# A tuned attention-then-FFN kernel on one core: the steps of its opening put in a new order, from the thirteenth on

## The chip, the cores and the metric

The kernel runs on one core of one Trainium2 chip. The metric is the device time of one execution in microseconds (us); several executions are taken and their median is compared.

The engines go by short names in the profile: PE is TensorE, PEld its weight loads, DVE is VectorE, ACT is ScalarE, POOL is GpSimd, SP is SyncE, which here only issues transfers. "SPq", "ACTq" and "POOLq" are the instruction streams from which an engine issues a transfer (DMA).

## The reference: what is computed

Eight batches with eight heads each, 576 queries and keys of 64 numbers per head, and 16 "beacon" keys and values per head put in front of the keys. Attention is causal for the 576 keys, the beacons are seen by all queries. The result of all heads (4608 tokens of 512 numbers) goes through a feed-forward part with three first matrices, of which the largest of three products is kept.

```
scores = scale * (q @ concat(beacon_k, k).T)      # causal for k, not for the beacons
a      = exp(scores - max);  a /= sum(a)
x      = a @ concat(beacon_v, v)                  # B x S tokens, H x D numbers
h      = maximum(maximum(x @ w1, x @ w2), x @ w3) # 512 -> 768
out    = h @ w_out                                # 768 -> 512
```

## The kernel before, in words

**Units of work.** Two heads make a pair, numbered over all batches: pairs 0 to 3 are batch 0, pairs 4 to 7 batch 1, 8 to 11 batch 2. Two pairs (four heads) make a quad: quads 0 and 1 are batch 0. The work is issued in an order that is written out by hand as a list of steps, `first_steps` (line 897) for the opening and `loop_steps` (line 1073) for the rest. Nothing plans at run time: each step appends its instructions to the in-order streams of the engines that it uses, and the engines wait for each other only where data or a buffer demands it. So the order of two steps matters for each engine that both use, and does not matter for the others. A step that issues transfers appends them to SP's or to GpSimd's stream, where they also stand in order.

**The steps**, with the lines that the profile names:

- `("load half", p, i, queue)`, line 219: the first half of the queries (i=0) or keys (i=1) of a pair, by SP or ScalarE; `("cast half", p, i, engine)`, line 227, makes it bf16. `("load quad half", g, h)`, line 236: half h of a quad's queries and keys, two transfers from GpSimd's stream, which convert on the way. `("load quad", b, g)`, line 245: the same for whole rows of a quad of batch b; it feeds the pairs of that quad ("whole").
- `("half", p, h, bank, q_copy, idle, idle_q)`, line 423: turns a half with TensorE (12 transposes, line 435) into two PSUM banks and copies queries and keys to SBUF (line 443). The keys are always copied by VectorE, the queries by the engine `q_copy`. `bank` is "pv" or "ffn". `idle_q` and `idle` are numbers of pairs of empty transposes (line 403) put in front of the queries and of the keys; they keep TensorE running where it would wait. `("whole", p, bank, q_copy)`, line 795, does it for all rows of a pair (24 transposes, line 384; copies, lines 448 and 459).
- `("load keys", ...)`, `("cast keys", ...)`, `("turn keys", ...)`: beacon keys of batch 0 (set 0) and of batches 1 to 3 (set 1), cast (lines 862 and 876) and turned by TensorE (line 355); ScalarE copies them out of PSUM (lines 361 and 362). `("keys", p, engine)`, line 455, places them in front of a pair's keys.
- `("scores", p, group, idle)`, line 498: `idle` empty matmuls (line 473), then the score matmuls of one of four groups of a pair (line 509), then the exponential of both heads on ScalarE (line 524), into the tile `at_sb`. The PSUM tile comes from a ring of two buffers ("sc"); `("widen",)` closes the pool of the FFN banks and adds a third buffer ("wide") to the ring.
- `("mask", p, group, engine)`, line 530: sets what a query may not see to zero, with up to three instructions, each either a product with a triangle on VectorE or an affine_select on GpSimd:

```
if dve:
    m = tri[0:n, None, x0 : x0 + hi - lo]
    nc.vector.tensor_mul(view, view, m.to_broadcast([n, 2, hi - lo]))   # line 541
else:
    nc.gpsimd.affine_select(out=view, in_=view, ...)                     # line 543
```

- `("load v0", t, gate)`, line 293, and `("cast v0", t, engine)`, line 317: one of five pieces of batch 0's values from SP's stream, and its cast to bf16 (line 323). `("load v", b, piece, gate)` loads three or two pieces of a later batch. `("load pair", p, gate)` loads queries and keys of a pair of batch 2 from SP's stream (line 202).
- `("values", quad, half, bank, ...)`, line 563: the matmuls of probabilities with ones (which form the sums) and with values (line 584), 44 for a quad's first half of rows and 76 for its second. It needs every mask of its two pairs, and the casts of the value pieces that it reads. `("invert",)`, line 598: ScalarE forms the reciprocals of the sums (lines 604 and 606). `("multiply",)`, line 610: three VectorE products (line 616) put the result in `xT`.
- `("ffn", bank, kind)`, line 821: the next unit of the feed-forward part of a kind: 0 and 1 are the first and second 256 tokens of the first block of 512 tokens (eight matmuls, line 665, then VectorE, lines 673 and 675). Units 1 to 3 of kind 0 use w1 of the reference, units 4 to 6 w2, units 7 to 9 w3. `("load w", i)`, line 333, loads one of these, i = 0, 1, 2, with two transfers from GpSimd's stream. `("load w_out", gate)` loads the last matrix.
- `("load", n, gate)`: the next n loads of a list of later ones.

**The gates.** A load with a gate first writes one number of its target on the named engine. So the transfer can't start before that engine has come to this point of its stream:

```
def load_first_v(t, gate=None):
    dst = v_stage(0, t)
    if gate:
        idle[gate].memset(dst[32:33, 0, 0:1], 0.0)
    load_v_tile(0, t, dst)
```

All transfers of SP's stream stand in order, so one that waits for its gate also holds those behind it. GpSimd's own transfers have no gates; they are issued when GpSimd has done the steps in front of them.

**Around the change.** The first twelve steps are the same in both kernels: they load the halves of pairs 0 and 1, keep TensorE running with empty matmuls until the first data are there (about 7 us), and load the first halves of quad 1. After the opening, `loop_steps` goes over the batches in a fixed pattern; the change does not touch it.

## Time and profile before

| what | value |
|---|---|
| median of 3 runs | 291.97 us (291.77 to 292.08) |
| the profiled execution | 292.01 us, of which 289.6 us are the span of the instructions |
| TensorE busy | 279.8 us (97%), 3704 matmuls |
| VectorE, ScalarE, GpSimd busy | 168.2, 145.2 and 121.9 us |
| granted TensorE clock | 0.999 of full |
| transfers | 45.30 MB, 156 GB/s over the span |

The "timeline" view lists instructions in order of time, runs of alike ones merged: start and length in us, engine, line, operation, what is written <- what is read, shape, number, and in brackets how long the engine was idle before and what ended it. The "DMA" view gives for each queue its packets, MB and the time of its packets as a share of 16 DMA engines, and for each issue its size and the time to landing; q0 holds the transfers from GpSimd's stream and q1 those of SP's.

### The profile page before, as it was taken

To read this page: it belongs to the slowest core of one execution; us is meant where nothing else is said; L and a number is where in the kernel's file an instruction comes from. 1 tells how busy PE (TensorE), PEld (TensorE's weight loads), DVE (VectorE), ACT (ScalarE), POOL (GpSimd) and SP (SyncE) were. 2 spreads that over 40 slices of the span, in tenths; PEclk is the share of its full clock that TensorE was granted. 3 is DMA by queue.
4 is the path that set the end of the run, shared out by engine and by line. 5 is a ranking of instruction groups with operands and counts; after the bars stand their busy time and mean duration, and the time that the engine had idled before them with its cause. 6 is when DMAs were issued, how large, how long until landed. Compare 5 with 4: busy or idle time off the path is not lost.

```text
span 289.6 us, 8831 instructions
## 1 busy us (share of the span) xinstructions
PE 279.8 (97%) x3704; PEld 160.6 (55%) x3729; DVE 168.2 (58%) x317; ACT 145.2 (50%) x248; POOL 121.9 (42%) x246
## 2 busy tenths in 40 slices
PE   8889999999999999999999999999999999999995
PEld 7656677754555554544555887445554545444442
DVE  1555677856675557565746655665556565373273
ACT  2886576854566564835484258525862552200300
POOL 3717416644476483638365546464523320000000
PEclk9999999999999999999999999999999999999999
DMA  8999999999999999999999999999991003002103
GB/s 131 168 179 183 219 198 234 221 205 219 235 204 187 148 197 164 199 170 219 201 181 157 223 192 194 139 167 187 253 163 75 2 2 144 3 0 82 65 0 146
DMA packets 118231, 45.30 MB, mean 156 GB/s; under 512 B 107312, under 2 KB 112944, under 8 KB 118192
## 3 DMA queue, kind: packets, MB, share of 16 engines
q1 hardware_dynamic: 111984, 39.20, 76.1%
q0 software_dynamic: 5648, 5.21, 11.9%
q8 instruction: 29, 0.48, 0.7%
q10 hardware_dynamic: 560, 0.33, 0.4%
q14 instruction: 10, 0.08, 0.1%
HBM read 35.13 MB, written 9.44 MB: 154 GB/s over the span
## 4 chain that ended last, share of the span: by engine, by line
PE 86%; DMA 4%; ACT 3%; DVE 2%; POOL 2%; issue 1%; ACTq 0%; POOLq 0%
PE pv L646 21%; PE sc L646 14%; PE wide L646 8%; PE sc L682 8%; PE sc L584 7%; PE pv L682 6%; PE sc L509 6%; PE pv L584 5%; PE wide L509 3%; DMA w_sb<-in_moe_w_dram 2%; DMA bk<-in_beacon_k_dram 2%; PE wide L682 1%; PE pv L665 1%; PE wide L584 1%; PE sc L665 1%
## 5 line engine op out<-in xcount | busy, mean ns | idle before, releaser
L524 ACT ACTIVATE at_sb<-sc 128x736 bf16<-128x736 f32 (+5 forms) x87 | 72.9, 863 | 62.9 <-PE sc L509 62.3
L543 POOL TENSOR_SCALAR_AFFINE_SELECT at_sb<-at_sb 128x256 bf16<-128x256 bf16 (+3 forms) x140 | 51.7, 387 | 105.7 <-ACT at_sb L524 104.7
L646 PEld LDWEIGHTS <-w_sb 128*128 128x128 bf16 x648 | 61.1, 98 | 60.7 <-issue 4.9
L646 PE MATMUL pv<-xT,w_sb 128*128 128x512 bf16 (+1 forms) x315 | 65.2, 347 | 0.3
L524 ACT ACTIVATE at_sb<-wide 128x672 bf16<-128x672 f32 (+3 forms) x41 | 35.1, 856 | 23.3 <-PE wide L509 23.1
L646 PE MATMUL sc<-xT,w_sb 128*128 128x512 bf16 (+1 forms) x202 | 44.1, 362 | 0.3
L656 DVE TENSOR_TENSOR hT<-hT,pv 128x512 bf16<-128x512 bf16 x48 | 32.4, 686 | 13.2 <-PE pv L646 13.2
L255 POOL CAST p<-st 96x768 bf16<-96x768 f32 x48 | 38.3, 824 | 3.4 <-DMA st<-in_k_dram 3.4
L682 PEld LDWEIGHTS <-hT 128*128 128x128 bf16 x210 | 19.6, 98 | 23.5 <-issue 1.1
L616 DVE TENSOR_TENSOR xT<-pv,recip 128x288 bf16<-128x288 f32 (+2 forms) x48 | 14.2, 350 | 26.5 <-ACT recip L606 26.5
L509 PE MATMUL sc<-qT,kT 64*128 64x288 bf16 (+6 forms) x286 | 26.8, 271 | 2.0 <-POOL at_sb L543 0.6
L509 PEld LDWEIGHTS <-kT 64*128 64x128 bf16 x400 | 14.8, 94 | 22.2 <-issue 12.8
L646 PE MATMUL wide<-xT,w_sb 128*128 128x512 bf16 (+1 forms) x113 | 26.1, 364 | 0.5 <-issue 0.2
L584 PEld LDWEIGHTS <-v_sb 128*32 128x32 bf16 (+1 forms) x1408 | 24.7, 96 | 2.3 <-issue 1.0
L682 PE MATMUL sc<-w_out_sb,hT 128*128 128x512 bf16 x103 | 24.4, 379 | 0.3
L656 DVE TENSOR_TENSOR hT<-hT,sc 128x1024 bf16<-128x1024 bf16 (+1 forms) x15 | 17.0, 1147 | 5.2 <-PE sc L646 5.0
L682 PE MATMUL pv<-w_out_sb,hT 128*128 128x512 bf16 x83 | 19.9, 380 | 0.1
L656 DVE TENSOR_TENSOR hT<-hT,wide 128x1024 bf16<-128x1024 bf16 (+1 forms) x11 | 12.3, 1120 | 10.8 <-PE wide L646 10.6
L311 POOL CAST v_sb<-st 128x1536 bf16<-128x1536 f32 (+2 forms) x21 | 18.4, 896 | 0.0
L654 DVE CAST hT<-pv 128x512 bf16<-128x512 f32 x20 | 13.7, 688 | 5.0 <-PE pv L646 5.0
L694 DVE COPY y<-sc 128x1024 f32<-128x1024 f32 (+1 forms) x10 | 11.2, 1118 | 8.7 <-PE sc L682 8.7
L616 DVE TENSOR_TENSOR xT<-sc,recip 128x288 bf16<-128x288 f32 (+2 forms) x39 | 11.5, 351 | 7.9 <-ACT recip L606 7.9
(115 smaller groups left out, 280.7 us busy)
## 6 DMA issues: line engine op xcount, KB each, us to landing
st<-in_q_dram SPq DMA_DIRECT2D x24, 288.0 KB, 5.6
st<-in_k_dram SPq DMA_DIRECT2D x24, 288.0 KB, 6.2
st<-in_v_dram SPq DMA_DIRECT2D x24, 256.0 KB, 5.8
out_dram<-y SPq DMA_DIRECT2D x9, 512.0 KB, 4.6
out_dram<-y SPq DMA_DIRECT2D x17, 256.0 KB, 3.0
w_sb<-in_moe_w_dram POOLq DMA_DIRECT2D x6, 384.0 KB, 7.0
st<-in_v_dram SPq DMA_DIRECT2D x8, 224.0 KB, 5.4
st<-in_v_dram SPq DMA_DIRECT2D x8, 160.0 KB, 4.3
```

The lines of the kernel that those rows point to most:

```text
L255: cast(t16.rearrange("p r h d -> p h r d"), st[0:QP, i * NQ2 : (i + 1) * NQ2].rearrange("p (h r d) -> p h r d", h=2, r=QR),)
L311: cast(v_sb[0:n, t:t1].rearrange("p t h d -> p (t h d)"), st[0:n, (t - t_lo) * H * D : (t1 - t_lo) * H * D],)
L509: nc.tensor.matmul(ps[:, e, off : off + q1 - q0], kT[hs, 128 * t : 128 * t + 128], qT[hs, q0:q1], start=True, stop=True, tile_position=(64 ...
L524: nc.scalar.activation(out=both_heads(p, gi), in_=ps[:, :, 0 : g_width(p, gi)], func=AF.Exp, scale=scale)
L543: nc.gpsimd.affine_select(out=view, in_=view, compare_op=ALU.is_ge, fill=0.0, base=x0, pattern=[[0, 2], [1, hi - lo]], channel_multiplier=-1,)
L584: nc.tensor.matmul(ps[bank][32 * j : 32 * j + 32, lo + q0 - qa : lo + qb - qa], lhsT, at_view(PPQ * quad + j // 2, t, j % 2, q0, qb), star ...
L616: nc.vector.tensor_mul(xT[:, 2 * g + part - 1, c0 + ca : c0 + cb], ps[bank][:, lo : lo + cb - ca], recip[:, ca:cb],)
L646: nc.tensor.matmul(dst[:, o0 : o0 + n], w_in[i][:, ct, 128 * (ft + f) : 128 * (ft + f + 1)], xT[:, ct, x0 : x0 + n], start=(ct == 0), stop ...
L654: (by_act if alone[0] else by_dve)(h, ps)
L656: nc.vector.tensor_max(h, h, ps)
L682: nc.tensor.matmul(ps[:, t - tt] if two else ps, hT[:, ft, 128 * t : 128 * (t + 1)], w_out_sb[:, ft, :], start=(ft == 0), stop=(ft == n_ft ...
L694: nc.vector.tensor_copy(y[:, 0:n], ps if two else ps[:, None])
```

## The change: a new order of the opening

The list has 164 steps from `("cast keys 0", "act")` to the last `("ffn", "pv", 1)` in both kernels, and the work in them is the same. What differs is the order, the engine of some steps, some PSUM banks, some gates and the numbers of empty matmuls. The diff:

```diff
@@ -908,166 +908,166 @@
         ("cast keys 0", "act"),
         ("load half", 1, 1, "sp"),
         ("cast half", 0, 0, "act"),
-        ("cast half", 1, 0, "act"),
-        ("load v0", 0, "dve"),
-        ("half", 0, 0, "ffn", "act", 0, 7),
-        ("cast half", 1, 1, "act"),
         ("turn keys 0",),
-        ("load v0", 1, "pool"),
-        ("keys", 3, "act"),
+        ("cast half", 1, 1, "pool"),
+        ("cast half", 1, 0, "dve"),
+        ("load v0", 0, "pool"),
+        ("load v0", 1, "dve"),
+        ("half", 0, 0, "pv", "act", 0, 8),
         ("load v0", 2),
+        ("half", 1, 0, "pv", "act", 3, 6),
         ("keys", 1, "act"),
-        ("keys", 2, "pool"),
+        ("keys", 3, "pool"),
+        ("scores", 0, 0, 0),
         ("load quad half", 0, 1),
-        ("half", 1, 0, "ffn", "act", 2, 9),
-        ("scores", 0, 0, 0),
-        ("scores", 1, 0, 3),
         ("load w", 0),
+        ("keys", 2, "act"),
+        ("half", 3, 0, "ffn", "dve", 0, 0),
+        ("scores", 1, 0, 0),
+        ("half", 2, 0, "pv", "act", 4, 0),
         ("cast v0", 0, "pool"),
-        ("half", 3, 0, "ffn", "act", 0, 0),
+        ("cast v0", 1, "act"),
         ("mask", 0, 0, "dve"),
-        ("cast v0", 1, "dve"),
-        ("half", 2, 0, "pv", "dve", 4, 0),
-        ("cast v0", 2, "act"),
-        ("scores", 3, 0, 3),
-        ("mask", 1, 0, "pool"),
+        ("mask", 1, 0, "dve"),
+        ("cast v0", 2, "dve"),
+        ("scores", 3, 0, 0),
+        ("load v0", 3, "pool"),
         ("scores", 2, 0, 6),
+        ("load keys 1",),
         ("values", 0, 0, "pv", 0, 4, 0),
-        ("half", 0, 1, "ffn", "act", 0, 7),
-        ("invert",),
-        ("load v0", 3, "dve"),
+        ("invert",),
+        ("mask", 2, 0, "pool"),
+        ("half", 0, 1, "ffn", "act", 0, 9),
         ("scores", 0, 2, 4),
+        ("scores", 0, 3, 0),
         ("mask", 3, 0, "dve"),
-        ("mask", 2, 0, "dve"),
-        ("scores", 0, 3, 0),
         ("multiply",),
         ("values", 1, 0, "ffn", 0, 4, 0),
         ("invert",),
-        ("half", 1, 1, "pv", "act", 0, 0),
+        ("mask", 0, 3, "dve"),
         ("multiply",),
         ("scores", 0, 1, 0),
-        ("mask", 0, 3, "dve"),
+        ("load v0", 4, "dve"),
         ("load quad half", 1, 1),
-        ("scores", 1, 2, 0),
-        ("load keys 1",),
-        ("load v0", 4, "dve"),
         ("mask", 0, 1, "pool"),
+        ("half", 1, 1, "pv", "act", 1, 0),
+        ("scores", 1, 2, 4),
+        ("ffn", "ring", 0),
+        ("mask", 0, 2, "dve"),
+        ("load w", 1),
+        ("cast keys 1", "pool"),
         ("ffn", "ffn", 0),
-        ("load w", 1),
-        ("mask", 1, 2, "dve"),
+        ("cast v0", 3, "act"),
+        ("scores", 1, 1, 0),
+        ("scores", 1, 3, 0),
+        ("half", 2, 1, "pv", "dve", 0, 0),
+        ("mask", 1, 3, "dve"),
         ("ffn", "ffn", 0),
-        ("mask", 0, 2, "pool"),
-        ("scores", 1, 3, 0),
-        ("half", 2, 1, "pv", "act", 0, 0),
-        ("scores", 1, 1, 0),
-        ("ffn", "ffn", 0),
-        ("mask", 1, 3, "pool"),
+        ("load v", 1, 0, "pool"),
         ("half", 3, 1, "pv", "dve", 0, 0),
         ("scores", 2, 3, 0),
-        ("cast v0", 3),
-        ("load quad", 1, 0),
         ("scores", 2, 2, 7),
-        ("cast v0", 4),
+        ("cast v0", 4, "dve"),
         ("scores", 3, 2, 0),
         ("mask", 1, 1, "dve"),
-        ("cast keys 1", "pool"),
+        ("mask", 1, 2, "dve"),
         ("values", 0, 1, "pv", 0, 4, 0),
         ("scores", 3, 3, 0),
-        ("load w", 2),
+        ("mask", 2, 3, "dve"),
         ("turn keys 1",),
+        ("keys", 5, "act"),
+        ("ffn", "ffn", 0),
+        ("mask", 3, 3, "dve"),
+        ("invert",),
+        ("mask", 2, 2, "dve"),
+        ("scores", 2, 1, 0),
+        ("load quad", 1, 0),
         ("keys", 4, "act"),
         ("ffn", "ffn", 0),
-        ("mask", 3, 3, "pool"),
-        ("load v", 1, 0, "pool"),
-        ("mask", 2, 3, "pool"),
-        ("invert",),
-        ("keys", 5, "act"),
-        ("scores", 2, 1, 0),
-        ("mask", 2, 2, "pool"),
-        ("multiply",),
-        ("ffn", "ffn", 0),
+        ("ffn", "ring", 0),
+        ("load w", 2),
         ("mask", 2, 1, "pool"),
+        ("multiply",),
+        ("load pair", 9, "pool"),
+        ("scores", 3, 1, 0),
+        ("mask", 3, 1, "dve"),
         ("mask", 3, 2, "pool"),
-        ("ffn", "ffn", 0),
-        ("scores", 3, 1, 1),
-        ("mask", 3, 1, "dve"),
         ("whole", 4, "ffn", "dve"),
+        ("values", 1, 1, "pv", 0, 4, 0),
+        ("invert",),
         ("widen",),
-        ("values", 1, 1, "pv", 0, 4, 0),
-        ("invert",),
-        ("scores", 4, 1, 0),
-        ("multiply",),
-        ("scores", 4, 2, 1),
-        ("whole", 5, "ring", "act"),
+        ("multiply",),
+        ("scores", 4, 1, 1),
+        ("scores", 4, 2, 0),
+        ("mask", 4, 1, "dve"),
+        ("whole", 5, "ring", "dve"),
         ("ffn", "ring", 1),
-        ("mask", 4, 1, "dve"),
         ("ffn", "ring", 1),
-        ("scores", 5, 0, 1),
+        ("mask", 4, 2, "dve"),
+        ("scores", 5, 0, 0),
+        ("ffn", "pv", 1),
         ("scores", 4, 0, 0),
-        ("load pair", 8, "dve"),
+        ("mask", 5, 0, "dve"),
         ("scores", 4, 3, 0),
+        ("ffn", "ring", 0),
+        ("load pair", 8, "pool"),
         ("ffn", "pv", 1),
-        ("ffn", "ring", 0),
-        ("ffn", "pv", 1),
+        ("scores", 5, 1, 0),
         ("scores", 5, 3, 0),
-        ("load pair", 9, "pool"),
-        ("mask", 5, 0, "dve"),
-        ("mask", 4, 2, "dve"),
-        ("mask", 5, 3, "dve"),
+        ("mask", 4, 3, "dve"),
         ("scores", 5, 2, 0),
         ("load quad", 1, 1),
-        ("mask", 4, 3, "dve"),
-        ("keys", 7, "act"),
-        ("scores", 5, 1, 0),
+        ("keys", 6, "pool"),
+        ("ffn", "pv", 0),
+        ("load v", 1, 1),
         ("mask", 4, 0, "pool"),
-        ("ffn", "pv", 0),
+        ("mask", 5, 3, "pool"),
+        ("mask", 5, 2, "pool"),
+        ("whole", 6, "ring", "dve"),
         ("ffn", "ring", 0),
-        ("load v", 1, 1),
+        ("cast v", 1, 0),
         ("load", 2, "dve"),
-        ("whole", 6, "ring", "dve"),
-        ("keys", 6, "pool"),
         ("ffn", "pv", 1),
-        ("mask", 5, 2, "pool"),
-        ("cast v", 1, 0),
+        ("load w_out", "dve"),
+        ("scores", 6, 1, 0),
+        ("scores", 6, 0, 0),
         ("scores", 6, 2, 0),
-        ("scores", 6, 1, 0),
         ("mask", 5, 1, "pool"),
-        ("scores", 6, 0, 0),
-        ("load w_out", "dve"),
-        ("ffn", "pv", 1),
-        ("load", 1),
-        ("values", 2, 0, "ring", 0, 4, 0),
-        ("invert",),
-        ("keys", 9, "act"),
-        ("cast pair", 8),
-        ("whole", 7, "ring"),
         ("mask", 6, 0, "pool"),
         ("ffn", "pv", 1),
-        ("multiply",),
+        ("whole", 7, "ring", "dve"),
+        ("load", 1, "dve"),
+        ("keys", 9, "act"),
+        ("load", 2, "pool"),
+        ("load", 1),
+        ("cast pair", 8),
+        ("keys", 7, "pool"),
+        ("values", 2, 0, "ring", 0, 4, 0),
+        ("ffn", "pv", 1),
+        ("invert",),
+        ("cast v", 1, 1),
+        ("scores", 6, 3, 0),
+        ("multiply",),
+        ("scores", 7, 2, 0),
+        ("whole", 8, "pv", "dve"),
         ("cast pair", 9),
-        ("load", 2, "dve"),
-        ("scores", 6, 3, 0),
-        ("scores", 7, 2, 0),
-        ("cast v", 1, 1),
-        ("whole", 8, "pv", "dve"),
-        ("load", 1, "pool"),
         ("scores", 7, 0, 0),
         ("mask", 6, 1, "dve"),
+        ("scores", 7, 1, 0),
+        ("values", 2, 1, "ring", 0, 4, 0),
+        ("mask", 7, 2, "pool"),
+        ("mask", 7, 1, "pool"),
+        ("invert",),
+        ("scores", 7, 3, 0),
+        ("mask", 6, 3, "pool"),
         ("mask", 7, 0, "dve"),
-        ("mask", 6, 3, "dve"),
-        ("scores", 7, 1, 0),
-        ("mask", 7, 1, "pool"),
-        ("mask", 7, 2, "pool"),
-        ("values", 2, 1, "ring", 0, 4, 0),
-        ("keys", 8, "pool"),
-        ("invert",),
-        ("mask", 6, 2, "dve"),
-        ("scores", 7, 3, 0),
-        ("load", 1, "dve"),
+        ("load", 1),
+        ("mask", 7, 3, "pool"),
         ("whole", 9, "ring", "act"),
-        ("multiply",),
-        ("mask", 7, 3),
-        ("load", 1),
+        ("keys", 8, "act"),
+        ("load", 1, "pool"),
+        ("multiply",),
+        ("mask", 6, 2, "pool"),
         ("ffn", "pv", 1),
     ]
     loop_steps = [
```

4 lines of the change are left out of this document (2 added, 2 removed).

## The prediction

> **What bounds the kernel now.** I read the page's first part, then the busy times by stage, then the timeline of the opening.
>
> ```profile
> PE 279.8 (97%) x3704; PEld 160.6 (55%) x3729; DVE 168.2 (58%) x317; ACT 145.2 (50%) x248; POOL 121.9 (42%) x246
> ...
> 10.00:60.00 50.00, 46.58 (x923) 33.41 (x926) 32.55 (x87) 36.20 (x60) 25.18 (x53) 1.00 1.13 200
> 60.00:70.00 10.00, 9.95 (x124) 5.27 (x114) 5.87 (x12) 4.43 (x8) 3.46 (x8) 1.00 1.03 215
> ```
>
> The columns of a stage are its length, the busy time of PE, PEld, DVE, ACT and POOL, the granted clock, the share of the DMA engines and GB/s. From 60 us on PE is full. Between 10 and 60 us it idles 50.00 - 46.58 = 3.42 us. The work on PE is the same in both orders except for empty matmuls. So the change is worth what it does to these 3.42 us and to the empty work, and whatever it has won or lost when the opening ends is carried, by a full PE, to the end. I therefore follow PE from one fixed point to the next:
>
> ```profile
> 14.07 0.52 PE L584 MATMUL pv<-at_sb,ones 128*32 128x288 bf16 x12
> ...
> 17.63 0.59 PE L584 MATMUL fps<-at_sb,ones 128*32 128x288 bf16 x12 [0.43 <-DVE at_sb L541]
> ...
> 20.77 1.91 PE L665 MATMUL fps<-xT,w_sb 128*128 128x256 bf16 x16 [0.26 <-DVE xT L616]
> ...
> 26.59 0.68 PE L584 MATMUL pv<-at_sb,ones 128*32 128x288 bf16 x20
> ...
> 35.37 0.33 PE L509 MATMUL sc<-qT,kT 64*128 64x288 bf16 x4
> ...
> 44.94 0.70 PE L384 MATMUL wide<-ident,whole 96*64 96x96 bf16 x24
> 45.58 1.05 PE L665 MATMUL pv<-xT,w_sb 128*128 128x256 bf16 x8
> 47.18 0.53 PE L509 MATMUL sc<-qT,kT 64*128 64x464 bf16 x6 [0.56 <-DVE qT L448]
> ```
>
> These are the starts of values 0 0 (14.07), values 1 0 (17.63), the first FFN unit (20.77), values 0 1 (26.59), the scores that follow values 1 1 (35.37), whole 6 (44.94), and the scores of pair 6 (47.18). An FFN unit takes 0.88 from start to start (eight of line 665), so the unit at 45.58 is through at 46.46, and PE waits 0.72 for VectorE's copies of whole 6.
>
> **The change part by part.**
>
> *To the first FFN unit.*
>
> ```profile
> 9.54 1.94 ACT L524 ACTIVATE at_sb<-sc 128x1024 bf16<-128x1024 f32 x2
> ...
> 12.15 0.99 PE L473 MATMUL sc<-busy 128*128 128x320 bf16 x6
> ...
> 12.40 1.29 POOL L543 TENSOR_SCALAR_AFFINE_SELECT at_sb<-at_sb 128x224 bf16<-128x224 bf16 x3
> ...
> 16.80 1.09 DVE L541 TENSOR_TENSOR at_sb<-at_sb,tri 128x224 bf16<-128x224 bf16 x6
> ...
> 18.95 0.41 ACT L604 ACTIVATE lnd<-fps 128x288 f32<-128x288 f32 x1 [0.48 <-PE fps L584]
> ...
> 19.54 0.46 DVE L443 COPY kT<-pv 128x288 bf16<-128x288 bf16 x1 [0.84 <-PE pv L435]
> ...
> 19.91 0.88 DVE L616 TENSOR_TENSOR xT<-fps,recip 128x288 bf16<-128x288 f32 x3
> ```
>
> The two halves of pairs 0 and 1 now both use the pv banks, so the second waits for the copies of the first, and the scores of pair 0 start about 0.15 later (9.25). That is repaid: ScalarE no longer stands behind a cast of pair 1, the exponentials 0 0 and 1 0 (0.97 each) end at 11.85 with one beacon copy between them, and six empty matmuls (0.95) and one score step bring values 0 0 to 13.2, if VectorE has finished masks 0 0 and 1 0 (0.55 each by the six in 1.09) and one cast by 12.9, which it has. Mask 2 0 on GpSimd (1.29, from 14.75) ends at 16.0, mask 3 0 on VectorE at 16.5; values 1 0 starts at 16.6, 1.0 earlier than now. Then most is given back. Today the half 1 1 is copied before the second multiply. Now VectorE does the multiply first, and half 1 1's keys are queued behind it; scores 1 2 waits for them, and on PE the FFN unit is queued behind scores 1 2. From the start of values 1 0: 1.32 until its sums are in PSUM, 0.88 for the two ScalarE steps (18.95 to 19.83), 0.80 multiply, 0.07 gate, 0.46 copy, 0.05 to PE, 0.32 scores: 16.6 + 3.9 = 20.5, against 20.77.
>
> The v pieces of batch 0 asked for sooner (piece 0 by 0.6 us, piece 3 by over 5) gain nothing by themselves. No row of today's casts waits for a landing.
>
> *To values 0 1.* The remaining masks and casts bind here. From the first FFN unit: two units and two score steps put exponential 1 3 at the end of a row of four ScalarE steps, at 24.2. VectorE's stream then has mask 1 3 (0.23), the third unit's cast (0.69), two copies (0.37 each from start to start), cast v0 4 (0.33), masks 1 1 and 1 2. 24.25 + 2.35 = 26.6, so the lead of 0.3 is gone.
>
> ```profile
> 25.87 0.62 POOL L323 CAST v_sb<-st 80x512 bf16<-80x512 f32 x1
> ...
> 25.95 0.70 DVE L541 TENSOR_TENSOR at_sb<-at_sb,tri 128x256 bf16<-128x256 bf16 x1
> ...
> 33.69 0.29 DVE L541 TENSOR_TENSOR at_sb<-at_sb,tri 128x256 bf16<-128x256 bf16 x1 [0.80 <-ACT at_sb L524]
> ```
>
> I take 0.29 for mask 1 1, since GpSimd has nothing to compute there in the new order; with a cast beside it it would be 0.70, 0.4 us more on the path. The Trainium skill, "SBUF — State Buffer", Who interferes with whom, says that a VectorE instruction with two SBUF inputs and a GpSimd instruction that reads SBUF lock each other out; the two rows agree (0.70 beside the cast, 0.29 without).
>
> *To the scores after values 1 1.* w2 is requested 1.4 us sooner (20.05 for 21.45), which saves this wait:
>
> ```profile
> 29.17 0.83 PE L665 MATMUL fps<-xT,w_sb 128*128 128x256 bf16 x6 [0.24 <-DMA w_sb<-in_moe_w_dram]
> ```
>
> But the multiply of values 0 1 now stands behind FFN units 5 and 6 on VectorE, and values 1 1 needs its banks. Units 5 and 6 end at 31.6, their two maxima at 32.45, multiply and mask 3 1 at 33.5 (33.7 by the row above). So values 1 1 starts and ends 0.2 earlier (**-0.2**), if whole 4, which stands before it on PE, has its data.
>
> *The transfers.* This is the costly part. GpSimd now comes early to its gates and its own transfers: v of batch 1 goes out at about 21.9 (29.77 now), the quad for pairs 4 and 5 at 21.95 to 23.4 (24.49), w3 at 23.4 (27.07), pairs 9 and 8 at about 32 (39.5), just ahead of the quad for pairs 6 and 7 (32.4; 32.15 now).
>
> ```profile
> 21.45 1.10 POOL L333 DMA_DIRECT2D w_sb<-in_moe_w_dram  x2
> ...
> 25.19 0.68 POOL L245 DMA_DIRECT2D whole<-in_k_dram  x1
> ...
> 29.77 3.45 SPq L275 DMA_DIRECT2D st<-in_v_dram  x3
> ...
> 39.51 0.33 SPq L202 DMA_DIRECT2D st<-in_q_dram  x1
> ...
> whole<-in_k_dram POOLq DMA_DIRECT2D x1, 288.0 KB, 6.8
> ...
> w_sb<-in_moe_w_dram POOLq DMA_DIRECT2D x2, 384.0 KB, 7.6
> ...
> q0 software_dynamic: 142, 0.38, 97.1%
> q1 hardware_dynamic: 79, 0.02, 6.2%
> ...
> q1 hardware_dynamic: 1638, 0.41, 106.5%
> q0 software_dynamic: 59, 0.07, 20.6%
> ...
> q0 software_dynamic: 360, 0.27, 91.4%
> q1 hardware_dynamic: 537, 0.14, 42.0%
> ...
> q1 hardware_dynamic: 732, 0.53, 113.9%
> ```
>
> The first four rows are issues: w2, the quad keys for 4 and 5, v of batch 1, pair 8. The next two give the time to landing of those quad keys (25.19 to 32.0) and of the two parts of w3 (issued 27.07 and 27.62, landed 33.9 and 36.0, 7.6 on average). The rows of the queues are the stages from 32, 34, 36 and 44 us, 2 us each. v of batch 1, issued from 29.77, got 6.2% while w3, issued before it, ran; from 34 it had the engines; from 36 it shared them with the quad issued 2.4 us after it, one to two. So what is asked for clearly earlier goes first, and neighbours share. Rates: w2's second part landed at 29.1 and two quad parts followed by 32.0, 1.45 each; w3's took 2.0 each; v 0.41 MB in 2 us, 3.5 us in all; pairs 0.53 MB in 2 us, 2.2 us each. In the new order w2 lands at 27.7. One piece of v (1.1) goes ahead, then the quad has two thirds: 2.9 / 0.67 = 4.35, and its keys land at 33.15. Whole 4 wants them at 32.2; it ends at 33.5, just when values 1 1 can start anyway.
>
> The rest of v (0.95) and w3 (4.0) follow until 38.1, then pair 9 (2.2) and the quad for 6 and 7 beside pair 8 (4.35): its keys land at 44.65. Now they land at 42.05, long before 44.94. If nothing of the pairs is ahead it is 42.45, and if all of them and a piece of batch 1's second v part (1.3) are, 38.1 + 4.4 + 2.9 + 1.3 = 46.7. I take the middle, since pair 9 alone is asked for clearly earlier.
>
> *To the end of the opening.* After values 1 1 there is one empty matmul for today's two (**-0.23**, by the gap between its start and that of the next scores). FFN units now stand on both sides of whole 6: 1.76 us of PE work between it and the scores of pair 6, against 1.44 that VectorE needs for two copies and some 0.3 around them. So the wait goes (**-0.72**). Whole 6 itself comes one unit earlier: 44.94 - 0.88 - 0.2 - 0.23 = 43.63, and its keys 0.33 later. They land at 44.65: **+0.7**.
>
> ```profile
> 38.46 0.10 PEld L473 LDWEIGHTS <-busy 128*128 128x128 bf16 x1
> 38.57 0.30 PE L473 MATMUL sc<-busy 128*128 128x320 bf16 x1
> ...
> 45.69 0.76 DVE L459 COPY kT<-wide 128x576 bf16<-128x576 bf16 x1
> ...
> 51.23 0.32 PE L509 MATMUL wide<-qT,kT 64*128 64x336 bf16 x2
> 51.84 0.37 PE L509 MATMUL sc<-qT,kT 64*128 64x464 bf16 x2 [0.30 <-ACT qT L448]
> ```
>
> In the last two rows PE waits some 0.34 for the queries of whole 7 (the scores at 51.23 take 0.27 to issue). Whole 7 now comes before values 2 0 and VectorE copies both parts, so this goes too (**-0.34**). GpSimd is late next: keys 7, cast v 1 1 and cast pair 9 stand behind cast pair 8, 1.6 us as now; I cost that at nothing, because PE gets there hardly earlier than today. The swapped beacon copies, casts and gates lie beside full PE work; without that cover each would cost its own 0.1 to 0.6.
>
> Sum on the profiled execution: -0.2 - 0.23 - 0.72 + 0.7 - 0.34 = -0.79, from 292.01 (a span of 289.6 and 2.4 around it, which the change does not touch) to 291.22; the median lies 0.04 lower: **291.2**.
>
> **The rivals.**
>
> *The transfers stay out of the way.* If the two queues share from the start, the quads land at 27.7 + 4.35 = 32.05 and at 42.45, both in time, and the +0.7 falls away: **290.5**. For it: the stage from 36. Against it: that from 32. The Trainium skill, "DMA: Bandwidth & Descriptors", Queues, rings and completion order, has each DMA engine go round its queue rows packet by packet; by that rule this rival would hold. The rows at 36 agree, those at 32 do not.
>
> *Slower: the quads' keys come last.* Place: the key transposes of whole 4 and whole 6 on PE. With strictly first come first served, all v is ahead of the first quad: 27.7 + 3.5 + 2.9 = 34.1; whole 4 ends at 34.45 and values 1 1 takes 1.65, so the scores start at 36.1 for 35.37 (+0.7). The second quad's keys land at 46.7 against 44.85: +1.8. Sum +0.7 - 0.23 - 0.72 + 1.8 - 0.34 = +1.2: **293.2**. It makes the change slower once the second keys land after about 45.8.
>
> *The change does not gain what it moves.* The lead of 1 us at values 1 0 is lost by 20.5 as shown; if VectorE, which holds more masks now, also holds the copies of whole 6 and 7, the gains of 0.72 and 0.34 shrink: **291.8**.
>
> **How the numbers follow.** A measurement of this kernel can tell about 0.2% (0.58 us) from no change: faster is below 291.39, slower above 292.55. Chances: 0.38 for the forecast (0.20 of it below 291.39, since my starts are good to some 0.5), 0.24 for the transfers out of the way, 0.30 for the slower rival, 0.08 for the last. So 0.44 faster, 0.26 same, 0.30 slower. The range reaches from below the first rival to near the second, 290.3 to 293.0.
>
> **What would show it.** Right: values 0 0 about 0.9 and values 1 0 about 1.0 earlier; the first FFN unit within 0.4 of 20.5; values 0 1 at 26.6; whole 6's transposes released by a DMA at about 44.7; no wait on VectorE's copies at the scores of pair 6. Wrong: the lead of 1 us kept past the first FFN unit (then VectorE's order did not bind), no DMA in front of whole 6 (first rival), or whole 4 and 6 both held for over 1 us (second). A granted clock below 1.00 in the opening would void all of it.

## The result, and the profile after

The changed kernel takes 290.02 us (median of 20 runs, 288.64 to 291.81), the kernel before, run beside it, 291.97 us (20 runs, 291.33 to 292.97). The ratio is 0.993, 95% interval 0.9916 to 0.9945: 1.6 to 2.5 us faster. The forecast was 291.2, with a range from 290.3 to 293.0. The direction is right; the time lies below the range.

Not all of the gain lies in the instructions that a trace shows. The record has the span of the instructions of each run. In the 20 runs of the changed kernel the time is 1.95 to 2.06 us longer than the span (2.01 on average); in 91 runs of the kernel before, taken beside the experiments, it is 2.13 to 2.49 longer (2.33). So some 0.3 us of the gain are won outside the span. What that time is, no run shows.

The profiled execution took 290.93 us (span 288.9), one of the longer ones. This is its page, then its busy times by stage:

```profile
PE 279.3 (97%) x3704; PEld 160.0 (55%) x3729; DVE 170.2 (59%) x320; ACT 143.5 (50%) x244; POOL 121.0 (42%) x247
```

```profile
10.00:60.00 50.00, 46.95 (x950) 33.48 (x946) 34.24 (x90) 36.27 (x61) 23.32 (x52) 1.00 1.10 197
60.00:70.00 10.00, 9.92 (x104) 5.04 (x97) 6.48 (x13) 3.83 (x6) 3.58 (x8) 1.00 1.07 220
```

Between 10 and 60 us PE idles 3.05 us, 0.37 less than before; from 60 us on it is as full as it was. What is won inside the span lies in the opening, but the idle time of this one execution shows only part of it. The timeline of PE at the forecast's points:

```profile
13.13 0.52 PE L584 MATMUL pv<-at_sb,ones 128*32 128x288 bf16 x12
...
16.26 0.52 PE L584 MATMUL fps<-at_sb,ones 128*32 128x288 bf16 x12
...
19.62 0.56 PE L509 MATMUL sc<-qT,kT 64*128 64x288 bf16 x4 [0.56 <-ACT qT L443]
20.11 1.35 PE L665 MATMUL sc<-xT,w_sb 128*128 128x256 bf16 x8
...
26.46 0.68 PE L584 MATMUL pv<-at_sb,ones 128*32 128x288 bf16 x20
...
31.87 0.45 PE L384 MATMUL fps<-ident,whole 96*64 96x96 bf16 x12
33.22 0.45 PE L384 MATMUL fps<-ident,whole 96*64 96x96 bf16 x12 [0.90 <-DMA whole<-in_k_dram]
33.59 0.68 PE L584 MATMUL pv<-at_sb,ones 128*32 128x288 bf16 x20
...
35.21 0.31 PE L473 MATMUL sc<-busy 128*128 128x320 bf16 x1
...
43.76 0.70 PE L384 MATMUL sc<-ident,whole 96*64 96x96 bf16 x24
44.39 1.05 PE L665 MATMUL sc<-xT,w_sb 128*128 128x256 bf16 x8
45.27 1.04 PE L665 MATMUL pv<-xT,w_sb 128*128 128x256 bf16 x8
46.24 0.33 PE L509 MATMUL wide<-qT,kT 64*128 64x288 bf16 x4
...
57.22 0.41 PE L584 MATMUL pv<-at_sb,ones 128*32 128x288 bf16 x12
```

The reader is to see three things. The values of quads 0 and 1 (values 0 0 and 1 0) start 0.9 and 1.4 us earlier. PE waits 0.90 for the keys of whole 4, which cancels the lead at the start of values 1 1. And whole 6 (43.76) meets no wait, nor do the scores of pair 6 behind it (46.24): the wait of 0.72 is gone and the forecast's wait for keys did not come.

One execution is not the kernel, so both were traced again (the runs `again`, `third_look` and `before_again` below). Start of each point in us:

| point | before | before again | after | again | third look | forecast |
|---|---|---|---|---|---|---|
| values 0 0 | 14.07 | 14.12 | 13.13 | 13.59 | 13.23 | 13.2 |
| values 1 0 | 17.63 | 17.68 | 16.26 | 16.72 | 16.36 | 16.6 |
| first FFN unit | 20.77 | 20.82 | 20.11 | 20.57 | 20.22 | 20.5 |
| values 0 1 | 26.59 | 26.64 | 26.46 | 26.30 | 25.95 | 26.6 |
| values 1 1 | 33.32 | 33.86 | 33.59 | 32.87 | 32.65 | 33.5 |
| end of values 1 1 | 35.37 | 35.91 | 35.21 | 34.49 | 34.26 | 35.2 |
| whole 6 | 44.94 | 45.49 | 43.76 | 43.08 | 42.84 | 43.6 |
| values 3 0 | 58.24 | 58.78 | 57.22 | 57.42 | 56.31 | |
| start of values 1 1 to values 3 0 | 24.92 | 24.92 | 23.63 | 24.55 | 23.66 | |
| end of values 1 1 to values 3 0 | 22.87 | 22.87 | 22.01 | 22.93 | 22.05 | 22.3 |
| span | 289.6 | 290.4 | 288.9 | 288.6 | 287.6 | |

The end of values 1 1 is where PE starts on what follows; the forecast's sum counts from there, with -0.2 ahead of it. The means give 33.59 against 33.04 at the start of values 1 1 (0.55 won ahead of it), 2.05 against 1.62 from its start to its end (0.43 won in it), and 22.87 against 22.33 behind it (0.54 won), 1.5 in all. What is won in values 1 1 shows in the old order's timelines of PE and of ScalarE:

```profile
33.32 1.02 PE L584 MATMUL pv<-at_sb,ones 128*32 128x288 bf16 x18
```

```profile
32.66 1.00 ACT L524 ACTIVATE at_sb<-sc 128x992 bf16<-128x992 f32 x1 [1.25 <-PE sc L509]
```

The matmuls for the sums take 1.02 there and 0.68 in the new order: after the first two PE goes on at 33.71, just behind the exponential of pair 3 that ends at 33.66. The profile names no releaser for this gap.

Waits for transfers move about: before, for expert weights near 28.9 us (0.24 and 0.73); after, at whole 4 (0.90), whole 6 (0.68) or hardly at all.

### The profile page after: what moved, and what is told of

It reads as the page before. It is cut to its first block, busy times and chain, and to the rows that moved or that the text cites. A ratio compares the mean times of both kernels' runs of the same rounds, so it can differ in the third digit from the quotient of the medians.

```text
span 288.9 us, 8832 instructions
## 1 busy us (share of the span) xinstructions
PE 279.3 (97%) x3704; PEld 160.0 (55%) x3729; DVE 170.2 (59%) x320; ACT 143.5 (50%) x244; POOL 121.0 (42%) x247
## 4 chain that ended last, share of the span: by engine, by line
PE 88%; DMA 6%; POOL 1%; issue 1%; SPq 1%; ACT 1%; DVE 0%; POOLq 0%
PE pv L646 21%; PE sc L646 15%; PE wide L646 8%; PE pv L682 6%; PE sc L509 6%; PE sc L682 5%; PE pv L584 4%; PE wide L682 4%; PE sc L584 4%; PE wide L584 4%; DMA whole<-in_k_dram 3%; DMA bk<-in_beacon_k_dram 3%; PE pv L665 3%; PE wide L509 2%; PE pv L473 2%
## 5 line engine op out<-in xcount | busy, mean ns | idle before, releaser
L524 ACT ACTIVATE at_sb<-sc 128x736 bf16<-128x736 f32 (+5 forms) x95 | 79.2, 866 | 61.4 <-PE sc L509 60.8
L646 PEld LDWEIGHTS <-w_sb 128*128 128x128 bf16 x648 | 61.1, 98 | 60.7 <-issue 4.9
L543 POOL TENSOR_SCALAR_AFFINE_SELECT at_sb<-at_sb 128x256 bf16<-128x256 bf16 (+2 forms) x138 | 50.9, 387 | 103.7 <-ACT at_sb L524 95.4
L646 PE MATMUL sc<-xT,w_sb 128*128 128x512 bf16 (+1 forms) x205 | 45.6, 363 | 0.7 <-issue 0.2
L656 DVE TENSOR_TENSOR hT<-hT,pv 128x512 bf16<-128x512 bf16 x48 | 32.4, 685 | 13.2 <-PE pv L646 13.2
L524 ACT ACTIVATE at_sb<-wide 128x736 bf16<-128x736 f32 (+3 forms) x33 | 28.0, 847 | 24.4 <-PE wide L509 22.4
L656 DVE TENSOR_TENSOR hT<-hT,sc 128x1024 bf16<-128x1024 bf16 (+1 forms) x19 | 20.8, 1104 | 12.6 <-PE sc L646 12.5
L646 PE MATMUL wide<-xT,w_sb 128*128 128x512 bf16 (+1 forms) x110 | 24.5, 364 | 0.1
L682 PE MATMUL sc<-w_out_sb,hT 128*128 128x512 bf16 x68 | 16.3, 380 | 0.2
L665 PEld LDWEIGHTS <-w_sb 128*128 128x128 bf16 x144 | 13.1, 98 | 3.4 <-issue 1.2
L606 ACT ACTIVATE recip<-lnd 128x288 f32<-128x288 f32 x32 | 14.2, 443 | 1.0
L694 DVE COPY y<-pv 128x512 f32<-128x512 f32 x14 | 9.7, 692 | 8.4 <-PE pv L682 8.0
```

What stands on the lines that cost most here:

```text
L524: nc.scalar.activation(out=both_heads(p, gi), in_=ps[:, :, 0 : g_width(p, gi)], func=AF.Exp, scale=scale)
L543: nc.gpsimd.affine_select(out=view, in_=view, compare_op=ALU.is_ge, fill=0.0, base=x0, pattern=[[0, 2], [1, hi - lo]], channel_multiplier=-1,)
L606: nc.scalar.activation(out=recip, in_=lnd, func=AF.Exp, scale=-1.0)
L646: nc.tensor.matmul(dst[:, o0 : o0 + n], w_in[i][:, ct, 128 * (ft + f) : 128 * (ft + f + 1)], xT[:, ct, x0 : x0 + n], start=(ct == 0), stop ...
L656: nc.vector.tensor_max(h, h, ps)
L665: nc.tensor.matmul(ps[:, f], w_in[i][:, ct, 128 * (ft + f) : 128 * (ft + f + 1)], xT[:, ct, tb * TOKB + lo : tb * TOKB + hi], start=(ct == 0),
```

## The experiments

My theory after the result: **A**, the gain lies behind values 1 1, where copies no longer hold PE, and transfers decide how much of it an execution shows. The rival: **B**, the earlier first FFN unit is kept to the end. Ratios are to the kernel before, run beside each group.

**Parts of the order.** The new steps up to a cut and the old ones behind it, or the reverse.

`again`: no edit.

> The changed kernel once more, to see whether another execution shows the same waits. Theory A (the gain sits in the stretch after values 1 1, about 1.1 us, and the rest of the 1.95 us in the median comes from transfers that land at other times in each execution): the TensorE wait for the quad's keys before whole 4, 0.90 us in the profiled execution of 290.93 us, differs by several tenths here, and the median stays near 290.0. Theory B (the gain is the earlier first FFN unit, 20.11 for 20.77, kept to the end): the time follows the start of that unit, and the wait before whole 4 does not matter.

`first_part`:

```
 new steps 1 to 48 (to the first FFN unit)
 old steps 49 to 164
```

> The new order only from the thirteenth step to the first FFN unit, the old order behind it. Theory A: the lead of 0.66 us at the first FFN unit is lost at values 0 1 (mask and cast chain on VectorE), so 291.7 to 292.0. Theory B: 0.6 to 0.7 us of it stay, 291.3.

`first_and_middle`:

```
 new steps to the first scores of pair 4
 old steps behind
```

> The new order up to the first scores of pair 4, the old order behind it. Theory A: 291.6 to 291.8 (a gain of 0.2 at the scores after values 1 1), with the 0.72 us wait for the copies of whole 6 still there. Theory B: 291.3. If the early requests for v of batch 1 and pair 9 are what counts, it is near 290.0 already.

`tail_part`:

```
 old steps to the scores after values 1 1
 new steps behind (and pair 9's request)
```

> The old order up to the scores after values 1 1, the new order behind it (pair 9 requested there). Theory A: -0.23 -0.72 -0.34 = -1.3 us, 290.7, with no wait of TensorE at the scores of pair 6. Theory B: 292.0.

Measured against a before of 292.26: `again` 290.59, ratio 0.9932 (0.9908 to 0.9956); `first_part` 291.34, 0.9965 (0.9949 to 0.9982); `first_and_middle` 291.53, 0.9981 (0.9963 to 0.9999); `tail_part` 291.81, 0.9975 (0.9956 to 0.9994). Part of this lies outside the span: the time is 2.32 longer than the span in the before of this group, 2.00 in `again`, 1.96 in `first_and_middle`, and 1.77 in both `first_part` and `tail_part` (averages). The spans by themselves are shorter by 1.78 in `again`, 0.46 in `first_part`, 0.30 in `first_and_middle` and 0.21 in `tail_part`, with two standard errors of 0.5 to 0.7. So of the 0.9 us that `first_part` wins in the median over half is not in its instructions, and `tail_part` wins nothing in them that can be told. Neither theory stands alone, and the parts do not add up to the whole. The timelines of PE in `first_part` and then in `first_and_middle` show what the old steps do with a lead:

```profile
46.53 0.37 PE L509 MATMUL sc<-qT,kT 64*128 64x464 bf16 x2 [0.55 <-DVE qT L448]
51.83 0.37 PE L509 MATMUL sc<-qT,kT 64*128 64x464 bf16 x2 [0.93 <-ACT at_sb L524]
```

```profile
46.89 0.37 PE L509 MATMUL wide<-qT,kT 64*128 64x464 bf16 x2 [0.55 <-DVE qT L448]
52.58 0.37 PE L509 MATMUL wide<-qT,kT 64*128 64x464 bf16 x2 [1.33 <-DVE xT L616]
```

The wait at the scores of pair 7, 0.30 before, has grown to 0.93 and 1.33: a lead runs into it. The new tail has neither wait. In the trace of `tail_part` the way from the start of values 1 1 to values 3 0 takes 24.17 for 24.92, though PE waits 0.39 at a later score.

**Single steps.** `whole6_only`, in the old order:

```
+("whole", 6, "ring", "dve"),
 ("ffn", "ring", 0),
 ...
-("whole", 6, "ring", "dve"),
```

> The old order, with whole 6 moved ahead of one FFN unit, so that 1.76 us of PE work lie between its transposes and the scores of pair 6; nothing else is changed. If the wait of 0.72 us for VectorE's copies is on the path and nothing takes its place: 0.6 us below the old order, 291.4 to 291.7, and no wait at the scores of pair 6. If the next wait, at the scores of pair 7 (0.3 us in the old order), grows by as much: within 0.2 us of the old order.

Measured: 291.96, ratio 0.999 (0.9972 to 1.0007). PE goes through to the scores of pair 6:

```profile
46.22 1.04 PE L665 MATMUL pv<-xT,w_sb 128*128 128x256 bf16 x8
47.19 0.53 PE L509 MATMUL sc<-qT,kT 64*128 64x464 bf16 x6
```

From values 1 1 (33.96 here, 33.32 before) to these scores it is 13.23 us where it was 13.86: the wait is gone, and the next one stays at 0.30. The times can't tell 0.6 from 0.

`copy_first`, in the new order:

```
+("half", 1, 1, "pv", "act", 1, 0),
 ("multiply",),
 ...
-("half", 1, 1, "pv", "act", 1, 0),
 ("scores", 1, 2, 4),
```

> The changed order with the half 1 1 moved back ahead of the second multiply, as it stood in the old order, so that VectorE copies its keys before it multiplies. The forecast's step (on VectorE the key copy stands behind the multiply, and PE waits for it at scores 1 2 with the first FFN unit behind) gives: no wait of 0.5 us at scores 1 2, the first FFN unit 0.3 to 0.4 us earlier against values 0 0, and the median 0.3 lower if that is kept (about 289.9), the same if the later copies and masks of VectorE take it back (290.2 to 290.5). If the multiply, now later, holds the FFN unit as long, the first FFN unit stands where it did.

Measured: 290.5, ratio 0.9945 (0.9921 to 0.9968). The first FFN unit starts 6.51 us after values 0 0 (20.16 - 13.65), where the changed order has 6.98 or 6.99 in its three traces. Values 0 1 follows after 12.64, against 12.71 and 12.72 in `again` and `third_look`. So the order of the copies does bind at the first FFN unit (the edit moves the copies of the queries and of the keys; which of them binds is taken up below). What is freed is gone by values 0 1, but not shown to be taken by VectorE's later copies and masks, as the expectation had it: in this trace ScalarE's cast of v piece 3 waits 0.24 for its landing, and PE 0.22 for the keys of a quad's half.

`quad_first`, in the new order:

```
+("load quad", 1, 0),
 ("cast keys 1", "pool"),
 ...
-("load quad", 1, 0),
```

> The changed order, with GpSimd's request for the queries and keys of pairs 4 and 5 moved from behind the FFN units after values 0 1 to the place ahead of the cast of the beacon keys of batch 1, so that it no longer stands behind a cast that waits for a landing (keys requested at about 22.5 us, not at 24.2). Theory A (the transfers' order sets the waits at whole 4 and whole 6): whole 4 starts without a wait for its keys, values 1 1 some 0.5 us earlier against values 0 0, median 289.6. Theory B (the lead is kept whatever the transfers do, the waits are hidden behind values 1 1 and the like): within 0.2 us of the changed order, 290.1 to 290.5. A third outcome, that the quad goes ahead of v piece 3 and the beacon keys, shows as a later values 0 1 and 290.8 or more.

Measured: 290.12, ratio 0.9918 (0.9892 to 0.9944). The wait at whole 4 is gone, but ScalarE's cast of v piece 3 waited 0.34 for its landing and values 0 1 came at 26.85. Nothing is won that the times can tell.

`late_v0`: the five requests for v pieces of batch 0 back at their old places.

```
-("load v0", 3, "pool"),
 ("scores", 2, 0, 6),
 ...
 ("half", 0, 1, "pv", "act", 0, 9),
+("load v0", 3, "dve"),
```

> The changed order with the five requests for v pieces of batch 0 moved back to their places in the old order (piece 3 behind values 0 0, piece 4 behind scores 1 2) and their gates on the old engines; everything else as changed. The forecast's step (the pieces asked for sooner gain nothing by themselves, since no cast waits for a landing): within 0.3 us of the changed order, 290.0 to 290.6. The rival (ScalarE now casts piece 3 some 2.5 us sooner than GpSimd did, and without the sooner request it waits for the landing, with the exponentials of block 1 behind it): the cast waits 1.5 us or more, values 0 1 that much later against the first transposes, and 290.9 to 291.8.

Measured: 290.36, ratio 0.9927 (0.9906 to 0.9948), no slower. These are SP's timeline and the DMA issues of a stage around the request for piece 3, in the changed kernel and then in `late_v0`:

```profile
11.69 0.37 SPq L275 DMA_DIRECT2D st<-in_v_dram  x1
...
st<-in_v_dram SPq DMA_DIRECT2D x1, 256.0 KB, 9.8
```

```profile
16.31 0.39 SPq L275 DMA_DIRECT2D st<-in_v_dram  x1
...
st<-in_v_dram SPq DMA_DIRECT2D x1, 256.0 KB, 5.3
```

Asked for 4.6 us later, the piece lands at 21.6 where it landed at 21.5: in this pair of traces the earlier request only waited longer. In `again` and `third_look` it landed at 20.95 and 20.5, before ScalarE came for it, while in `late_v0` the cast waited 0.42. So the sooner request can spare a wait of some 0.4 us, which the times can't tell, and the 1.5 or more of the rival did not come.

**The dealing of masks and casts.** `old_engines`: the new order, 17 steps on their old engines.

```
-("mask", 1, 3, "dve"),
+("mask", 1, 3, "pool"),
...
-("mask", 2, 2, "dve"),
+("mask", 2, 2, "pool"),
```

> The changed order of steps, with the masks, the casts of halves and the casts of v pieces of the opening dealt to the engines of the old order (17 steps, among them masks 1 0, 0 2, 1 3, 2 3, 3 3 and 2 2 back on GpSimd). The forecast's view (the six masks on VectorE cost what they save, values 0 1 stands where it did): 290.0 to 290.8. The rival (the dealing is what brings values 0 0 and 1 0 forward: GpSimd's mask takes some 0.4 us where VectorE's takes 0.18, and stands behind gates and casts): values 0 0 and 1 0 0.4 us or more later against the first transposes, 290.8 to 292.

Measured: 295.93, ratio 1.0123 (1.01 to 1.0146), slower than before. Both expectations fell short. GpSimd's timeline, then PE's:

```profile
29.27 0.60 POOL L543 TENSOR_SCALAR_AFFINE_SELECT at_sb<-at_sb 128x160 bf16<-128x160 bf16 x2 [2.85 <-ACT at_sb L524]
29.83 0.70 POOL L245 DMA_DIRECT2D whole<-in_q_dram  x1
```

```profile
34.33 0.45 PE L384 MATMUL fps<-ident,whole 96*64 96x96 bf16 x12 [1.62 <-DMA whole<-in_q_dram]
35.85 0.45 PE L384 MATMUL fps<-ident,whole 96*64 96x96 bf16 x12 [1.07 <-DMA whole<-in_k_dram]
```

GpSimd waits 2.85 us for an exponential, masks, and only then requests the quad, 6.3 us later than in the changed kernel (23.56, by the row further down).

`old_engines_quad`: that kernel with the quad requested ahead of `("cast keys 1", "pool")`.

> The changed order with the old dealing of masks and casts (295.9 us), and GpSimd's request for the queries and keys of pairs 4 and 5 moved ahead of the cast of the beacon keys of batch 1 and of the masks. In the old dealing the request went out at 29.83 us, behind that cast's wait and six of GpSimd's masks and casts; PE waited 1.62 at whole 4 and 1.07 at whole 5. Theory A (the dealing costs by holding GpSimd's requests): the request goes out at about 22, both waits vanish, and the median falls by 2 to 3 us, to 293 or 294. Theory B (it costs by the masks' own length): the median falls by less than 0.8 us.

Measured: 294.16, ratio 1.0065 (1.0037 to 1.0093). Both waits vanished and 1.8 us came back, a little under theory A's two to three. Some 4 us over the changed order remain: values 0 0 at 13.54, waits on PE of 0.72, 1.18 and 0.55 at later places. So the late request is about a third of what the old dealing costs. The rest is not split up by any run. Part of it goes with the clock: the five runs with a granted clock of 0.994 or less took 294.3 to 296.2, the other five 292.5 to 294.0.

`new_engines`: the old order, the same 17 steps on their new engines.

> The old order of steps with the new dealing of masks and casts (the same 17 steps), the other half of the change by itself. If the dealing brings the gain by freeing GpSimd, the quad for pairs 4 and 5 goes out sooner than at 24.5 us in the old order, and the median is 291.2 to 291.9. If the dealing pays only in the new order, because the old one is laid out for masks on GpSimd beside VectorE: 292 to 294.

Measured: 299.9, ratio 1.0249 (1.0213 to 1.0285), far above both expectations. Up to values 1 1 it shows the gain: values 0 0 at 13.32, the first FFN unit at 19.64, 1.1 us ahead of before. Then one mask spoils it. GpSimd's timeline and PE's:

```profile
43.31 0.49 POOL L543 TENSOR_SCALAR_AFFINE_SELECT at_sb<-at_sb 128x256 bf16<-128x256 bf16 x1 [11.19 <-ACT at_sb L524]
43.75 0.70 POOL L245 DMA_DIRECT2D whole<-in_q_dram  x1
```

```profile
50.16 0.69 PE L384 MATMUL wide<-ident,whole 96*64 96x96 bf16 x12 [5.49 <-DMA whole<-in_q_dram]
52.99 0.69 PE L384 MATMUL wide<-ident,whole 96*64 96x96 bf16 x12 [2.14 <-DMA whole<-in_k_dram]
```

Mask 5 3, on GpSimd in the new dealing, stands ahead of the request for the second quad in the old order and behind it in the new one. The order and the dealing are one change; neither half can be judged alone.

**Pair 9.** `pair9_late` and, once more, `pair9_again`:

```
-("load pair", 9, "pool"),
 ("scores", 3, 1, 0),
 ...
 ("load quad", 1, 1),
+("load pair", 9, "pool"),
```

> The changed order with the request for pair 9 moved from ahead of whole 4 to behind the request for the queries and keys of pairs 6 and 7. The forecast had pair 9 ahead of these keys in the queues, which would land 2.2 us sooner without it (42.1 us and not 44.3). Theory A (a queue of 256-byte packets takes little from one of large packets, whoever was first): the keys land where they did, at 42.2 to 42.6 in four of five traces, and the median is 290.0 to 290.6. Theory B (pair 9's bytes are in the way in some executions, such as the one where PE waited 0.68 at whole 6): the keys land below 41.5, and the median comes 0.2 to 0.4 lower, 289.6 to 289.9.

> The changed order with the request for pair 9 behind that for the queries and keys of pairs 6 and 7, a second time (289.40 in the first). If pair 9 costs what it takes from those keys: 0.3 to 0.7 us below the changed order on the same chip, the keys landing below 41.8 us. If the first run was lucky with its starts: within 0.2 us of the changed order.

`both_requests` (with `quad_first`'s edit as well) and `third_look` (no edit) ran beside the latter:

> Pair 9 requested behind the queries and keys of pairs 6 and 7, and the queries and keys of pairs 4 and 5 ahead of the cast of the beacon keys: every request of the quads taken out of the way of something that waits. If the waits at whole 4 and whole 6 are what is left of the transfers: no wait at either, 289.0 to 289.6, and the least scatter. If the earlier quad delays v piece 3 and the beacon keys as it did alone (0.34 us at the cast): as pair 9 alone.

> The changed order once more, on the same chip as the two below, for a third trace of it: median 290.0 to 290.6; the keys for whole 6 land between 42.2 and 44.2 us; a wait for a transfer at one of whole 4, whole 6 or the cast of v piece 3, not the same as before.

Measured: `pair9_late` 289.4, ratio 0.9907 (0.9882 to 0.9932); `pair9_again` 289.46, 0.9916 (0.9883 to 0.9949); `both_requests` 289.83, 0.9917 (0.9887 to 0.9947); `third_look` 289.6, 0.991 (0.9879 to 0.9941). On one chip they are the same: pair 9 is not what delays those keys, and no version beats the changed kernel by an amount that can be told. The third look came out below its expected 290.0 to 290.6, and in `both_requests` PE still waited 0.28 at whole 4, where no wait was expected.

**The start.** `fewer_empty` and `empty8`, in the new order:

```
-("busy", 12, 213),
+("busy", 4, 213),
```

(`empty8` has 8 there.)

> The changed order with 4 for 12 empty matmuls of 213 columns ahead of the first transposes. The 39 empty matmuls of the start took 5.4 to 6.4 us in six traces, by the moment at which a matmul's step goes from 0.167 to 0.083 us, and the first transposes start right behind them (6.76 to 7.76). If they hold the first transposes, these start at about 6.7 in any execution, values 0 0 at 12.6, and the median comes 0.3 to 0.6 below the changed order (289.5 to 289.9), with less scatter. If the casts and landings hold them, or if PE, left idle, is granted its short step later, it is as the changed order or slower (290.2 or more).

> The changed order with 8 for 12 empty matmuls ahead of the first transposes. With 4 the median came 0.5 us lower, but in the profiled execution PE idled 0.85 us and was granted half its clock from 8.9 to 15.5 us. If fewer empties pay by themselves: 289.6 to 289.9, the first transposes at 6.7 to 7.4, idle below 0.5 us and a clock of 1.00. If it is the idle time that brings the half clock at any length: a clock below 1.00 in the opening and 290 to 292. If nothing: 290.0 to 290.6.

Measured: 289.51, ratio 0.9903 (0.9875 to 0.9931), and 290.32, 0.9931 (0.9907 to 0.9955). Neither can be told from the changed order.

`before_again`, a second trace of the old order:

> The old order once more, for a second trace of it: the first transposes stood at 7.02 us in the first trace, earlier than in five of seven traces of other orders. If the start is a matter of the execution and not of the order, it stands elsewhere here (up to 7.8), while values 0 0 and 1 0 keep their distance from it (7.05 and 10.61 us) to 0.15; the waits for transfers (0.25 us for the expert weights at 28.9) may change by up to 1 us.

Measured: one run of 292.76; its points stand in the table. Values 0 0 and 1 0 stand where they stood (14.12, 17.68), while the first empty transposes stood earlier (6.62 for 7.02): in these two traces PE then waits for a cast (0.38 here) or has it just in time, so the start does not bind. A later start does: in `tail_part`, with the old opening, they stood at 7.58 and values 0 0 came at 14.51.

## Why the prediction was wrong, step by step

**To the first FFN unit: right, with one link more.** 0.87 was forecast at values 0 0 and 0.78 measured (means), 1.0 and 1.2 at values 1 0. The giving back is there: PE waits 0.56 at scores 1 2 in all three traces, and `copy_first` takes it away. But the profile has this wait ended by ScalarE's copy of the queries, which the forecast left out. The timelines of ScalarE, VectorE and PE in the changed kernel:

```profile
19.18 0.39 ACT L443 COPY qT<-pv 128x288 bf16<-128x288 bf16 x1
```

```profile
19.46 0.46 DVE L443 COPY kT<-pv 128x288 bf16<-128x288 bf16 x1
```

```profile
19.97 0.21 PE L509 MATMUL sc<-qT,kT 64*128 64x80 bf16 x2
```

The queries are there at 19.57 and the first two score matmuls start. VectorE's copy of the keys, the forecast's link, ends at 19.92, and the last two start at 19.97. So VectorE does come last, as forecast, but only 0.35 behind ScalarE. The lead left at the first FFN unit is 0.50 for a forecast 0.27.

**The v pieces sooner gain nothing: open.** "No row of today's casts waits for a landing" no longer holds in the new order, since ScalarE now wants piece 3 at 21.0, 2.9 us before GpSimd cast it (23.94). In the changed kernel it waited:

```profile
21.59 0.62 ACT L323 CAST v_sb<-st 128x512 bf16<-128x512 f32 x1 [0.58 <-DMA st<-in_v_dram]
```

In `again` and `third_look` the same cast waits for nothing.

**To values 0 1: "so the lead of 0.3 is gone" failed.** The forecast let VectorE's masks and casts bind here: 2.35 us from mask 1 3 to values 0 1. `third_look` took 1.88 (24.07 to 25.95) and the changed kernel 2.19, because the first matmuls of values 0 1 do not stand behind the last masks. VectorE's timeline in `third_look`:

```profile
25.89 0.58 DVE L541 TENSOR_TENSOR at_sb<-at_sb,tri 128x256 bf16<-128x256 bf16 x3
```

These masks end at 26.47, half a microsecond after values 0 1 has started. What binds is PE itself: it is busy for all of the 5.73 us from the first FFN unit to values 0 1 in `again` and in `third_look`, and was for all of the 5.82 before. So a lead at the FFN unit stays a lead (0.64 in `third_look`, 0.29 in `again`, whose start was later), unless a transfer takes it: the changed kernel, where the cast waits 0.58 and the keys of a half come late, needs 6.35 us and has 0.13 left. The mean lead is 0.38, against the mean of the two traces before.

At the end of values 1 1 the forecast had -0.2. From the first trace of before the three traces have -0.16, -0.88 and -1.11: the lead of values 0 1, the wait for w2, and the wait in values 1 1. In the changed kernel the keys of whole 4 landed at 33.1 and values 1 1 started at 33.59, near the forecast's 33.15 and 33.5. In the other two these keys landed at 31.9 and 32.1, and values 1 1 started at 32.87 and 32.65, so it could start well ahead of the 33.5 at which the forecast has it "anyway". In `again` it stands right behind the multiply (PE waits 0.46 for it), as forecast, but not behind mask 3 1, which runs on VectorE from 32.90.

**The empty matmul, the copies of whole 6 and the queries of whole 7: the waits go, but for less.** The terms -0.23, -0.72 and -0.34 sum to -1.29. From the end of values 1 1, where the sum counts from, the changed kernel is 0.86 and `third_look` 0.82 shorter than before. By term, in the changed kernel: 0.14 to whole 6 (one FFN unit of 0.88 taken into account), 0.64 from there to the scores of pair 6, and 0.08 from these to values 3 0. The wait of 0.30 for the queries of whole 7 is gone, but most of it is given back close behind: the transposes of pair 8 take 0.90 where they took 0.68.

**The transfers: the second step that failed.** It put +0.7 on whole 6, with the keys landing at 44.65, "the middle" between 42.45 and 46.7. GpSimd's timeline and the issues from 30.7 to 36 us in the changed kernel:

```profile
23.56 0.69 POOL L245 DMA_DIRECT2D whole<-in_q_dram  x1
...
32.71 0.68 POOL L245 DMA_DIRECT2D whole<-in_k_dram  x1
```

```profile
whole<-in_k_dram POOLq DMA_DIRECT2D x1, 288.0 KB, 9.6
```

They landed at 42.3 (32.71 + 9.6), at 40.9 in `third_look` and at 44.2 in `again`; of the three, only in `again` did PE wait for them (0.68). The second part of w3 landed at 37.5, 36.1 and 36.7 in these three, where the forecast has 38.1, and from there the keys took 4.8, 4.8 and 7.5, where it has 2.2 for pair 9 and 4.35 for the quad. So in two of three pair 9 did not go ahead of the keys. I had let what was asked for earlier go first, and neighbours share two to one, from one row of bytes. Here are both queues in 28 to 32 us, when v of batch 1 runs beside the quad and w3, in `again` and then in `third_look`:

```profile
q0 software_dynamic: 644, 0.63, 93.5%
q1 hardware_dynamic: 639, 0.16, 30.5%
```

```profile
q0 software_dynamic: 589, 0.66, 95.1%
q1 hardware_dynamic: 587, 0.15, 28.1%
```

The columns are packets, MB and share of the engines. In these two stages the queues took a packet each, and GpSimd's were about four times as large (1.0 KB for 0.25), so bytes went four to one. That is the rule that I had set aside, the Trainium skill, "DMA: Bandwidth & Descriptors", Queues, rings and completion order: each DMA engine goes round its queue rows packet by packet. By those four packet counts it holds. It doesn't say all: the changed kernel itself had 620 packets to 884 in that stage, and other stages are uneven too. The stage from 36 to 38 us, in `again` and in `third_look`:

```profile
q1 hardware_dynamic: 437, 0.15, 37.5%
```

```profile
q1 hardware_dynamic: 127, 0.03, 10.8%
```

Where the keys landed late (44.2 in `again`, 44.1 in `pair9_again` with 0.16 MB), q1 got five times what it got in `third_look`. This stage does not decide it alone: `empty8` and `both_requests` have 0.03 MB there and landed at 42.1 and 42.0. Why one execution lets the small packets in at that moment and another doesn't stays open; pair 9's place in the queue, by `pair9_again`, is not the reason.

**The time around the span: the third step that failed.** The forecast took "a span of 289.6 and 2.4 around it, which the change does not touch". In the changed kernel 2.0 lie around it, in each of 20 runs; in the first trace of before it is 2.4, and 2.33 on average. No run shows why.

**The sum.** Changes from the first trace of before, in us:

| term | forecast | after | again | third look | mean |
|---|---|---|---|---|---|
| to the end of values 1 1 | -0.20 | -0.16 | -0.88 | -1.11 | -0.72 |
| to whole 6 (empty matmuls) | -0.23 | -0.14 | -0.10 | -0.11 | -0.12 |
| whole 6 to the scores of pair 6 | -0.72 + 0.70 | -0.64 | +0.24 | -0.63 | -0.34 |
| to values 3 0 | -0.34 | -0.08 | -0.08 | -0.08 | -0.08 |
| around the span | 0 | -0.4 | -0.4 | -0.4 | -0.4 |
| sum | -0.79 | -1.4 | -1.2 | -2.3 | -1.7 |

The mean sum takes the 292.01 of the first trace to 290.3; the three traced executions took 290.4 on average, 0.35 above the median of 290.02. The wait for keys was paid in one of three traces (there it made 0.88 of difference). The three terms for the empty matmul, the copies and the queries, taken too high, hid part of what the lead and the transfers were taken too low: without this luck the forecast would have been further off. My first rival, transfers out of the way at 290.5, came in two of three traces, and still lies 0.5 above the measured time. My evidence against it was bytes where I should have counted packets (142 to 79 in the row at 32). The slower rival did not come: in no trace of the changed kernel did the second keys land after 45.8.

**What the forecast did not see** is what the dealing is worth. It counted masks by their lengths. `old_engines_quad` and `new_engines` show that a mask or cast on GpSimd can cost by what is queued behind it, a request. Beyond the 1.8 us that one moved request gave back, the cost of the old dealing is not explained.
